# Scan and mixture of experts on one core: the padding write and two half experts' weight loads move back in SyncE's queue

## The chip, the core and the metric

The kernel runs on one core of a Trainium2 chip. The core has five engines that run side by side, each through its own list of instructions in order: TensorE (PE, matrix products), VectorE (DVE), ScalarE (ACT), GpSimd (POOL) and SyncE (SP, which here only issues transfers). Transfers are carried by 16 DMA engines. The metric is the device time of one execution in microseconds (us); lower is better.

## What is computed

The first half is a gated scan over a sequence, the second a mixture of 8 experts, each token going to one expert:

```python
f = lower_bound + (1.0 - lower_bound) / (1.0 + np.exp(-f_logit))
for t in range(S):                        # 4 sequences of S = 5056, D = 256
    h = f[:, t] * h + (1.0 - f[:, t]) * x[:, t];  y[:, t] = h
logits = y @ w_gate;  e_idx = argmax(logits);  gate_w = softmax(logits)[e_idx]
eom = 1.0 / (1.0 + np.exp(-(y @ w_output_gate)))
for e in range(8):                        # N = 20224 tokens, F = 1024
    out[mask] = gate_w * eom[e] * (np.maximum(y[mask] @ w1[e], 0.0) @ w2[e])
```

## The kernel before

The 20224 tokens are cut into chunks of 512, with channels on the partitions. A chunk goes through these steps: load of `f_logit` and `x` (L236, L237, 512 KB each), tanh on ScalarE (L251), a product on VectorE (L255), the forget gate on ScalarE (L260), the scan on VectorE (L266), the norm (L273 and L277), a scale that is a power of two (`pow2`, L142 to L150), the split of the result into two float16 parts (L296 on ScalarE, L300 on VectorE), transposes by DMA into rows of tokens (`turn`, L293, four per chunk, 131 KB each), the gate products on TensorE (L311, L316, tile `pr`), the choice of expert in some twenty small VectorE instructions (from L328, tile `lgo`, to L410, which writes the tokens' factors into the rows), and four scatters by GpSimd (L413) that write the rows to their expert's region of a scratch array in DRAM, `scr`.

The rows of a chunk stand in one of three buffers: chunk 0 has a place of its own (`row0`, lent from the weights' tile `w1s`), odd chunks use `rows1`, even ones `rows0`. Chunk 3's transposes therefore write over the rows that chunk 1's scatters read. Chunk 0's inputs are lent the place `w2s`, chunk 3's the place `w1s`.

The experts' weights come in 16 half experts: `w1` of an expert, then its `w2`. A half is loaded by two transfers of 512 KB (`prep_load`, L546). TensorE forms products of it for its norm (`prep_gram`, L558, 16 products), VectorE takes them up (L565), and a scale follows. ScalarE and VectorE split the half into two float16 parts (L594, L599). The loop over `j` from -2 to 15 takes the halves in order: in step `j` half `j` is split, the products of half `j + 2` are formed and half `j + 3` is loaded. Beside each step some chunk stages run (`step`). As soon as 3 chunks have been scattered, first tiles of 128 tokens of each expert are gathered (`gather`, L607 to L613) and computed on the weights where they stand (L697 and the following); a second such round follows after 5 chunks. Later tiles work on copied weights (L655 and the following).

`padt` is one block of 128 padding rows with factor 0. It is written behind all regions of `scr` at the start (L211); an expert that has fewer than 128 rows yet gathers these rows.

What sets the order: SyncE issues its transfers exactly as the program text has them. For the other four engines, up to a cut, a scheduler orders the instructions by its own estimate of times; so another order in the text, or another place of a load, gives another order on those engines. At most eight of SyncE's transfers are under way: each waits for the one eight places before it.

The part around the change:

```python
    fresh.append(nc.sync.dma_start(out=scr[FREE : FREE + P, :], in_=padt))   # L211
    ...
    for n in range(min(EARLY[0], NCH)):          # L854: chunks 0, 1, 2
        load_chunk(n)
        if n:
            prep_load(n - 1)                     # half experts 0, 1
    for n in range(min(EARLY[0], NCH) - 1, deep):
        prep_load(n)                             # half experts 2, 3
```

Of the kernel before, what the change touches and what calls it, by code (L numbers as in the profile page):

```python
# [27 lines left out]
PERIOD = 8  # L28
# [3 lines left out]
EARLY = (3, 5)  # L32
# [18 lines left out]
def tile_scan_moe(  # L51
# [10 lines left out]
    nc = tc.nc  # L62
    P = 128
# [8 lines left out]
    NCH = -(-N // CH)  # L72
    R = N + P
    FREE = E * R
# [9 lines left out]
    def sure(tokens):  # L84
        """tiles of 256 tokens of one expert that any routing of so many tokens fills beside the first tiles"""
        return max(0, -(-(tokens - len(EARLY) * E * P - E * 255) // 256))
# [9 lines left out]

# [1 line left out]
    ident = cp.tile([P, P], F32, name="ident")  # L98
# [35 lines left out]
    def pow2(ss, t, nm):  # L134
        """from a norm's square: s, a power of two with s times the norm below 2 ** t, and 2 / s"""
        w = ss.shape[1]
        v = sp.tile([P, w], F32, tag=nm + "v", name=nm + "v", bufs=3)
        vi = v.bitcast(I32)
        sc = sp.tile([P, w], F32, tag=nm + "s", name=nm + "s", bufs=3)
        iv = sp.tile([P, w], F32, tag=nm + "i", name=nm + "i", bufs=3)  # L140
        yield SMALL
        nc.vector.tensor_scalar(v, ss, 2.0**-100, 2.0**120, ALU.max, ALU.min)  # L142
        yield SMALL
        nc.vector.tensor_scalar(vi, vi, EXPO, 1, ALU.bitwise_xor, ALU.logical_shift_right)
        yield SMALL
        nc.vector.tensor_scalar(vi, vi, EXPO, None, ALU.bitwise_and)
        yield SMALL
        nc.vector.tensor_scalar(sc, v, 2.0 ** (62 + t), None, ALU.mult)
        yield SMALL
        nc.vector.tensor_scalar(iv.bitcast(I32), sc.bitcast(I32), EXPO, None, ALU.bitwise_xor)  # L150
        return sc, iv

    def together(tasks):
        """a stage of each task: small instructions of VectorE that wait for one another alternate with others"""
        at = {id(g): (g, next(g, None)) for g in tasks}
        last = None
        while True:
            todo = [(g, kind) for g, kind in at.values() if kind]
            if not todo:
                return  # L160
            best = [x for x in todo if x[1] == SMALL and x[0] is not last]
            best = best or [x for x in todo if x[1] == BIG] or todo
            g = best[0][0]
            last = g if best[0][1] == SMALL else None
            del at[id(g)]
            at[id(g)] = (g, next(g, None))

    def alone(g):
        """runs a task to its end; what it returns"""
        while True:  # L170
            try:
                next(g)
            except StopIteration as end:
                return end.value

    # gate weights: the sum of two float16 parts of a scaled value
    gsq = cp.tile([P, KD * G], F32, name="gsq")
# [15 lines left out]

    # writes to rows of their own need no order among them; a reader waits for those it reads
    fresh = []

    def apart(ins, group, keep=()):
        tc.declare_no_dep(raw(ins), group=group, keep=[raw(k) for k in keep], reason="rows apart")
        tc.add_to_no_dep_group(group, raw(ins))

# [1 line left out]
    w1s = cp.tile([P, E, NF, KD, 2, P], F16, name="w1s")  # L202
# [3 lines left out]

    # rows behind each expert's rows: factor 0, an index no scatter takes
    padt = cp.tile([P, RW], I16, name="padt")
    nc.gpsimd.memset(padt, 0)
    nc.gpsimd.iota(padt[:, CM + 2 : CM + 4].bitcast(I32), pattern=[[0, 1]], base=N, channel_multiplier=0)  # L210
    fresh.append(nc.sync.dma_start(out=scr[FREE : FREE + P, :], in_=padt))  # L211
    apart(fresh[0], "scr")
    row2 = [cp.tile([P, NB, RW], I16, name=f"rows{i}") for i in range(2)]
    # the places of the last experts' weights serve the first chunks until then
    top1 = w1f[:, (E - 1) * 2 * WH : E * 2 * WH]
# [6 lines left out]

# [1 line left out]
    state = {"carry": None, "cnt": boff, "sent": boff}  # L224
# [15 lines left out]
    def chunk(c):  # L240
        """the steps of a chunk; each takes from the steps before what other engines made there"""
        t0 = c * CH
# [177 lines left out]

# [1 line left out]
    done0 = cp.tile([P, E], F32, name="done0")  # L422
    nc.gpsimd.memset(done0, 0.0)
    sched = {"done": done0, "new": []}
    slots = []
# [3 lines left out]
    def plan_first():  # L429
        """for each expert: its next 128 rows, or the free rows behind all regions where it has fewer yet"""  # L430
        done = sched["done"]
# [24 lines left out]
    def plan(k, nb, last):  # L456
# [41 lines left out]
        if last:  # L498
            # slots past the last tile take the rows behind expert 0's
            ends = t8("ends", I32)  # L500
# [99 lines left out]

# [1 line left out]
    mpool = {}  # L602
# [85 lines left out]

    # the first tile of an expert: its weights are read where they stand
    def first1(T, h):  # L690
# [46 lines left out]

# [1 line left out]
    prog = {"begun": 0, "tick": 0, "done": 0, "left": 0.0, "planned": 0, "final": False, "got": 0, "rounds": 0}  # L739
# [7 lines left out]
    def loading(c):  # L747
        """the steps of chunk c, with the load of the next once the chunk before has freed its place"""
        at = 0
        for kind in chunk(c):  # L750
            if not kind:
                at += 1
                if at == LOADAT and EARLY[0] <= c + 1 < NCH:
                    load_chunk(c + 1)
            yield kind
# [16 lines left out]
    def pump(tasks, need):  # L772
        """a stage of each chunk under way beside the tasks; every PERIOD stages one more begins"""
        if prog["tick"] <= 0 and prog["begun"] < NCH:
# [37 lines left out]
    def early(j):  # L812
        """half a first tile of an expert ready in step j: what VectorE does, and the rest"""
        if not line or line[0]["half"] == 1 and len(line) == 1:
# [39 lines left out]
    for n in range(min(EARLY[0], NCH)):  # L854
        load_chunk(n)
        if n:
            prep_load(n - 1)
    for n in range(min(EARLY[0], NCH) - 1, deep):
        prep_load(n)
    for j in range(-2, nh):  # L860
        tasks = []
        if 1 <= j < nh + 1 - deep:
            prep_load(j - 1 + deep)
# [28 lines left out]
    def ordered(start, cut):  # L892
        """up to cut the scheduler orders what the engines do, except SyncE"""
        loose = [e.engine for e in (nc.vector, nc.scalar, nc.tensor, nc.gpsimd)]
# [49 lines left out]
    ordered(0, prog["cut"])  # L944
    # the counts may leave the last tiles without a token
    if len(cuts) > 1:
# [43 lines left out]
```

## Time and profile before

| what | value |
|---|---|
| device time, median of 3 runs | 1019.66 us (1018.59 to 1021.29) |
| span of the profiled execution | 1016.9 us |
| busy: TensorE / VectorE / ScalarE / GpSimd | 911.9 / 887.5 / 511.4 / 376.5 us |
| moved by DMA | 146.34 MB, mean 144 GB/s |

The page gives the profiled execution's time as its span, first instruction to last; the runs' median lies 2.8 us above it. In a row of the timeline stand the start (us from the span's start), the time it takes, the engine, the line of the kernel, the operation, what is written and what is read, how often, and in brackets how long the engine had been idle and what ended that. `SPq` and `ACTq` are transfers issued by SyncE and ScalarE; their time is that of the issue, not of the transfer. Matrix products are named PE. `DMA_TRANSPOSE` is a transpose by DMA. In a row of waits stand the waiting instruction, what released it, the time in total, how often, and the longest.

### The profile page before, as it was taken

The numbers are of one execution on the slowest core, as the hardware profiler recorded it, in microseconds if no ns is written. First come the engines' busy times: TensorE is split into PE (matmuls) and PEld (weight loads), VectorE is DVE, ScalarE is ACT, GpSimd is POOL, SyncE is SP. The second block draws the span as 40 slices with busy tenths as digits, with TensorE's granted clock in tenths as the row PEclk, the third lists the DMA queues.
The fourth block names the chain that finished last, engine by engine and source line by source line (L and its number), as shares of the span: only waits on it lengthen the run. The fifth ranks groups of instructions, "written<-read, shape, count | busy, mean of one in ns | idle before, by whom it ended". The sixth has DMA issues, their size and how long they took to land.

```text
span 1016.9 us, 27437 instructions
## 1 busy us (share of the span) xinstructions
PE 911.9 (90%) x9775; PEld 822.8 (81%) x9775; DVE 887.5 (87%) x2803; ACT 511.4 (50%) x1075; POOL 376.5 (37%) x378
## 2 busy tenths in 40 slices
PE   2268998899999999999999999999999999999993
PEld 2157887788888888888888888888888888899993
DVE  7989896899999999999999999999999998758781
ACT  5667774545545555455455554454455543333331
POOL 1523234343444444433444434344444344221221
PEclk9999999999999999999999999999999999999997
DMA  8899966755566565555565565555665534312120
GB/s 309 202 308 287 267 153 154 179 137 138 138 141 151 135 149 153 137 138 137 137 149 141 157 145 132 139 135 132 149 144 152 138 85 104 95 49 45 47 55 16
DMA packets 238547, 146.34 MB, mean 144 GB/s; under 512 B 202558, under 2 KB 204224, under 8 KB 238401
## 3 DMA queue, kind: packets, MB, share of 16 engines
q1 hardware_dynamic: 222752, 101.74, 43.2%
q0 software_dynamic: 15360, 42.74, 13.7%
q8 instruction: 80, 1.31, 0.6%
q14 instruction: 67, 0.54, 0.2%
q10 hardware_dynamic: 288, 0.02, 0.0%
HBM read 58.38 MB, written 44.49 MB: 101 GB/s over the span
## 4 chain that ended last, share of the span: by engine, by line
DVE 54%; issue 17%; DMA 11%; PE 10%; POOL 3%; ACT 2%; SPq 1%; DVEq 1%; POOLq 0%; ACTq 0%
DVE hl L667 11%; DVE xt L266 7%; DVE w L637 5%; DMA rows<-ft 5%; DVE w L643 4%; DVE xt L255 4%; DVE ft L300 3%; POOL out_dram L732 2%; PE ph L655 1%; PE ph L657 1%; PE ph L656 1%; DMA xq<-scr 1%; PE py L685 1%; PE py L687 1%; PE py L686 1%
## 5 line engine op out<-in xcount | busy, mean ns | idle before, releaser
L655 PE MATMUL ph<-xq,w 128*128 128x256 f16 (+1 forms) x1312 | 331.0, 261 | 0.3 <-DVE xv L142 0.3
L657 PE MATMUL ph<-xq,w 128*128 128x256 f16 (+1 forms) x1312 | 331.2, 261 | 0.0
L656 PE MATMUL ph<-xq,w 128*128 128x256 f16 (+1 forms) x1312 | 331.1, 261 | 0.0
L685 PE MATMUL py<-w,hh 128*128 128x256 f16 x1168 | 318.6, 273 | 0.5 <-ACT ft L296 0.3
L687 PE MATMUL py<-w,hl 128*128 128x256 f16 x1168 | 318.6, 273 | 0.0
L686 PE MATMUL py<-w,hh 128*128 128x256 f16 x1168 | 318.5, 273 | 0.0
L732 POOL DMA_INDIRECT out_dram<-yo,mt x146 | 167.9, 1150 | 298.8 <-ACT yo L728 275.1
L413 POOL DMA_INDIRECT scr<-rows,dst x154 | 175.4, 1139 | 229.3 <-issue 215.5
L659 ACT ACTIVATE hh<-ph 128x512 f16<-128x512 f32 (+1 forms) x328 | 178.7, 545 | 153.1 <-PE ph L657 152.8
L667 DVE SCALAR_TENSOR_TENSOR hl<-ph,hh 128x512 f16<-128x512 f32 (+1 forms) x328 | 204.6, 624 | 10.9 <-ACT hh L659 9.1
L655 PEld LDWEIGHTS <-w 128*128 128x128 f16 x1312 | 128.0, 98 | 12.4 <-DVE w L637 0.6
L637 DVE COPY w<-w1s 128x2048 f16 x164 | 115.1, 702 | 26.1 <-PE ph L657 24.7
L657 PEld LDWEIGHTS <-w 128*128 128x128 f16 x1312 | 128.1, 98 | 11.7
L656 PEld LDWEIGHTS <-w 128*128 128x128 f16 x1312 | 128.1, 98 | 11.4
L687 PEld LDWEIGHTS <-hl 128*128 128x128 f16 x1168 | 114.2, 98 | 13.2
L686 PEld LDWEIGHTS <-hh 128*128 128x128 f16 x1168 | 114.2, 98 | 13.2 <-issue 0.8
L685 PEld LDWEIGHTS <-hh 128*128 128x128 f16 x1168 | 114.2, 98 | 12.5
L643 DVE COPY w<-w2s 128x2048 f16 x164 | 111.8, 682 | 0.5 <-PE py L687 0.3
L260 ACT ACTIVATE ft<-ft,fb,fa 128x512 f32<-128x512 f32 (+1 forms) x76 | 60.6, 807 | 100.7 <-DVE xt L255 98.0
L296 ACT ACTIVATE ft<-xt,sa 128x512 f16<-128x512 f32 (+1 forms) x76 | 50.2, 708 | 106.1 <-DVE li L285 101.9
L266 DVE TENSOR_TENSOR_SCAN xt<-ft,xt 128x512 f32<-128x512 f32 (+4 forms) x78 | 90.7, 1170 | 0.0
L728 ACT ACTIVATE yo<-py,fac 128x256 f32<-128x256 f32 x146 | 61.6, 465 | 26.4 <-PE py L687 25.7
(178 smaller groups left out, 1311.5 us busy)
## 6 DMA issues: line engine op xcount, KB each, us to landing
ft<-in_fT_dram SPq DMA_DIRECT2D x37, 512.0 KB
xt<-in_xT_dram SPq DMA_DIRECT2D x37, 512.0 KB
w<-in_wT_dram SPq DMA_DIRECT2D x32, 512.0 KB
scr<-rows,dst POOLq DMA_INDIRECT x154, 3.3
rows<-ft SPq DMA_TRANSPOSE x152
out_dram<-yo,mt POOLq DMA_INDIRECT x146, 2.8
xq<-scr SPq DMA_TRANSPOSE x99
scr<-padt SPq DMA_DIRECT2D x9, 136.0 KB
```

Of the source, the lines that this page charges most:

```text
L266: nc.vector.tensor_tensor_scan(out=xt[:, k, a:z], data0=ft[:, k, a:z], data1=xt[:, k, a:z], initial=init, op0=ALU.mult, op1=ALU.add)
L413: ins = nc.gpsimd.indirect_dma_start(out=scr[:, :], out_offset=IOA(ap=dst[:, b : b + 1], axis=0), in_=rows[:, b, :], in_offset=None)
L637: nc.vector.tensor_copy(out=w, in_=w1f[:, ds(T["ev"] * (2 * WH) + h * 2 * QH, 2 * QH)])
L655: nc.tensor.matmul(out=o, lhsT=w[:, f, k, 0, :], rhs=T["xh"][:, k, 0:n], start=first, stop=False)
L656: nc.tensor.matmul(out=o, lhsT=w[:, f, k, 0, :], rhs=T["xl"][:, k, 0:n], start=False, stop=False)
L657: nc.tensor.matmul(out=o, lhsT=w[:, f, k, 1, :], rhs=T["xh"][:, k, 0:n], start=False, stop=last)
L659: nc.scalar.activation(hh[:, :, 0:n], ph[:, :, 0:n], AF.Relu)
L667: nc.vector.scalar_tensor_tensor(out=hl[:, :, 0:n], in0=ph[:, :, 0:n], scalar=0.0, in1=hh[:, :, 0:n], op0=ALU.max, op1=ALU.subtract)
L685: nc.tensor.matmul(out=o, lhsT=hh[:, i, c], rhs=w[:, f, 0, :], start=first, stop=False, skip_group_check=True)
L686: nc.tensor.matmul(out=o, lhsT=hh[:, i, c], rhs=w[:, f, 1, :], start=False, stop=False, skip_group_check=True)
L687: nc.tensor.matmul(out=o, lhsT=hl[:, i, c], rhs=w[:, f, 0, :], start=False, stop=last, skip_group_check=True)
L732: ins = nc.gpsimd.indirect_dma_start(out=out[:, :], out_offset=IOA(ap=T["mt"][:, b, 2:4].bitcast(I32), axis=0), in_=T["yo"][:, b, :], in_o ...
```

## The change

The padding write moves from ahead of the first loads to behind them. The loads of half experts 2 and 3 move from ahead of the loop into its steps -1 and 0. Some texts in quotes or comments are gone as well; they make no instruction. Two lines fewer stand ahead of most of the code, so L236 of before is L234 now, L293 is L291, L410 is L408, L599 is L597, and so on.

```diff
@@ the padding block
     nc.gpsimd.iota(padt[:, CM + 2 : CM + 4].bitcast(I32), pattern=[[0, 1]], base=N, channel_multiplier=0)
-    fresh.append(nc.sync.dma_start(out=scr[FREE : FREE + P, :], in_=padt))
-    apart(fresh[0], "scr")
@@ ahead of the loop, and its first lines
         load_chunk(n)
         if n:
             prep_load(n - 1)
-    for n in range(min(EARLY[0], NCH) - 1, deep):
-        prep_load(n)
+    fresh.append(nc.sync.dma_start(out=scr[FREE : FREE + P, :], in_=padt))
+    apart(fresh[0], "scr")
     for j in range(-2, nh):
         tasks = []
-        if 1 <= j < nh + 1 - deep:
+        if -1 <= j < nh + 1 - deep:
             prep_load(j - 1 + deep)
```

The front of SyncE's queue before, up to the first transposes (`w` is a weight buffer, `w2s`, `ft` and `xt` the places of chunks' inputs):

```order
L211 DMA scr<-padt 128x544
L236 DMA w2s<-in_fT_dram 128x2x512
L237 DMA w2s<-in_xT_dram 128x2x512
L236 DMA ft<-in_fT_dram 128x2x512
L237 DMA xt<-in_xT_dram 128x2x512
L546 DMA w<-in_wT_dram 128x1024 x2
L236 DMA ft<-in_fT_dram 128x2x512
L237 DMA xt<-in_xT_dram 128x2x512
L546 DMA w<-in_wT_dram 128x1024 x6
L293 DMA_TRANSPOSE w1s<-w2s 128x4x128 x4
```

and now:

```order
L234 DMA w2s<-in_fT_dram 128x2x512
L235 DMA w2s<-in_xT_dram 128x2x512
L234 DMA ft<-in_fT_dram 128x2x512
L235 DMA xt<-in_xT_dram 128x2x512
L544 DMA w<-in_wT_dram 128x1024 x2
L234 DMA ft<-in_fT_dram 128x2x512
L235 DMA xt<-in_xT_dram 128x2x512
L544 DMA w<-in_wT_dram 128x1024 x2
L856 DMA scr<-padt 128x544
L291 DMA_TRANSPOSE w1s<-w2s 128x4x128 x4
```

The padding write went behind the weights, and four of the eight weight transfers left the front.

They stand again further on in SyncE's queue. Before, from the transposes of chunk 1 (`rows_133`) over those of chunk 2 (`rows_132`) and chunk 3 (`rows_133` again, from `w1s`) to the first gather (`xq`):

```order
L293 DMA_TRANSPOSE rows_133<-ft 128x4x128 x4
L293 DMA_TRANSPOSE rows_132<-ft 128x4x128 x4
L236 DMA ft<-in_fT_dram 128x2x512
L237 DMA xt<-in_xT_dram 128x2x512
L293 DMA_TRANSPOSE rows_133<-w1s 128x4x128 x4
L236 DMA ft<-in_fT_dram 128x2x512
L237 DMA xt<-in_xT_dram 128x2x512
L546 DMA w<-in_wT_dram 128x1024 x2
L607 TENSOR_LOAD pf_tab
L607 ISA x2
L610 ISA
L610 DMA_TRANSPOSE xq<-scr 128x4x128
```

and now, up to half expert 4 (chunk 1's and 3's rows are `rows_132` here, chunk 2's `rows_131`):

```order
L291 DMA_TRANSPOSE rows_132<-ft 128x4x128 x2
L544 DMA w<-in_wT_dram 128x1024 x2
L291 DMA_TRANSPOSE rows_132<-ft 128x4x128 x2
L291 DMA_TRANSPOSE rows_131<-ft 128x4x128 x4
L234 DMA ft<-in_fT_dram 128x2x512
L235 DMA xt<-in_xT_dram 128x2x512
L291 DMA_TRANSPOSE rows_132<-w1s 128x4x128 x2
L544 DMA w<-in_wT_dram 128x1024 x2
L291 DMA_TRANSPOSE rows_132<-w1s 128x4x128 x2
L234 DMA ft<-in_fT_dram 128x2x512
L235 DMA xt<-in_xT_dram 128x2x512
L544 DMA w<-in_wT_dram 128x1024 x2
```

Half expert 2 now stands in the midst of chunk 1's transposes and half expert 3 in the midst of chunk 3's, ahead of chunk 5's load and the first gather.

VectorE around the factors of chunk 0 (L410 before; it writes into the rows that GpSimd scatters first). Before:

```order
L300 SCALAR_TENSOR_TENSOR ft<-xt,sa,ft 128x512 x2
L340 TENSOR_REDUCE mx<-lgo 128x4
L404 SCALAR_TENSOR_TENSOR fc<-es,eg 128x4
L396 TENSOR_REDUCE dst<-pos 128x4
L343 TENSOR_TENSOR dl<-lgo,mx 128x32
L408 RECIPROCAL fc<-fc 128x4
L346 SCALAR_TENSOR_TENSOR key<-dl,rev 128x32
L410 TENSOR_SCALAR w1s<-fc,xi 128x4
L352 TENSOR_REDUCE km<-key 128x4
L399 TENSOR_REDUCE es<-ex 128x4
L255 SCALAR_TENSOR_TENSOR w1s<-w1s 128x512 x2
```

and now (L253, L264, L298, L326 and L408 are L255, L266, L300, L328 and L410 of before):

```order
L298 SCALAR_TENSOR_TENSOR ft<-xt,sa,ft 128x512 x2
L353 TENSOR_TENSOR oh<-key,km 128x32
L402 SCALAR_TENSOR_TENSOR fc<-es,eg 128x4
L264 SCALAR_TENSOR_TENSOR w1s<-w1s,xt 128x512 x2
L356 TENSOR_TENSOR og<-oh,lgo 128x32
L406 RECIPROCAL fc<-fc 128x4
L563 SCALAR_TENSOR_TENSOR jk,l_624<-pg,ident 128x128
L381 TENSOR_TENSOR pos<-pk,cnt 128x32
L387 TENSOR_TENSOR cnt<-cnt,pk 128x8
L326 TENSOR_TENSOR lgo<-lgp 128x64
L359 TENSOR_REDUCE gs<-og 128x4
L408 TENSOR_SCALAR w1s<-fc,xi 128x4
```

Chunk 0's factors now stand behind chunk 3's two scans (L264), behind the norm of half expert 2 (L563) and behind the first step of chunk 2's choice (L326); chunk 3's L253 pair stands ahead of these rows as well. On TensorE the 16 products of half expert 2 stand, in the new order, behind the first two of chunk 2's gate products and ahead of the others.

## The prediction

> **What bounds the kernel now.** I read the page first, for how busy the engines are over the span.
>
> ```profile
> span 1016.9 us, 27437 instructions
> PE   2268998899999999999999999999999999999993
> DVE  7989896899999999999999999999999998758781
> ...
> w<-in_wT_dram SPq DMA_DIRECT2D x32, 512.0 KB
> ```
>
> Each digit is 25.4 us. From the eighth slice on TensorE is at 9 of 10 and VectorE as well; in the first two slices TensorE is at 2 and VectorE nearly full. The order of the instructions of VectorE, ScalarE, TensorE and GpSimd differs from before only in the start, up to the first tiles of the later phase. So the change is decided in the first 60 us, and by how much of what it does there is still there at 180 us. The times by stretch (engine busy us, then clock, DMA share, GB/s) say what is short there.
>
> ```profile
> 10.00:19.00 9.00, 2.40 (x20) 1.86 (x19) 8.05 (x23) 7.79 (x17) 0.00 (x0) 1.00 1.04 417
> 23.00:26.00 3.00, 1.96 (x25) 1.80 (x23) 3.00 (x10) 1.38 (x5) 0.00 (x0) 1.00 1.40 208
> 26.00:30.00 4.00, 2.31 (x39) 2.04 (x35) 3.93 (x22) 3.49 (x8) 0.00 (x0) 1.00 1.02 278
> 30.00:38.00 8.00, 1.58 (x22) 1.07 (x23) 8.00 (x35) 5.12 (x12) 3.50 (x3) 1.00 1.06 164
> 60.00:110.00 50.00, 43.03 (x581) 40.26 (x581) 45.70 (x146) 35.38 (x61) 15.17 (x14) 0.97 1.07 288
> 110.00:160.00 50.00, 45.58 (x657) 42.39 (x654) 43.58 (x145) 35.49 (x63) 20.44 (x20) 1.00 0.73 189
> 160.00:180.00 20.00, 16.29 (x217) 15.14 (x217) 13.02 (x54) 9.17 (x19) 7.95 (x8) 0.91 0.83 169
> ```
>
> VectorE (third pair) is the full engine from 10 to 38 us; the DMA engines are full too. Then SyncE's queue in order of time, which holds the moved transfers:
>
> ```profile
> 3.16 0.38 SPq L211 DMA_DIRECT2D scr<-padt  x1
> 3.60 0.42 SPq L236 DMA_DIRECT2D w2s<-in_fT_dram  x1
> 7.77 6.55 SPq L546 DMA_DIRECT2D w<-in_wT_dram  x6
> 19.40 5.30 SPq L293 DMA_TRANSPOSE w1s<-w2s  x4
> 24.75 0.57 SPq L236 DMA_DIRECT2D w1s<-in_fT_dram  x1
> 25.93 10.89 SPq L293 DMA_TRANSPOSE rows<-ft  x8
> 37.01 0.44 SPq L236 DMA_DIRECT2D ft<-in_fT_dram  x1
> 46.35 5.15 SPq L293 DMA_TRANSPOSE rows<-w1s  x4
> 51.61 0.52 SPq L236 DMA_DIRECT2D ft<-in_fT_dram  x1
> 53.04 0.93 SPq L546 DMA_DIRECT2D w<-in_wT_dram  x2
> 55.08 1.21 SPq L610 DMA_TRANSPOSE xq<-scr  x1
> ...
> SPq L293 <- DMA scr<-rows,dst: 8.2, 2, 6.8
> SPq L211 <- POOL rows L378: 2.7, 1, 2.7
> POOL scr L413 <- DMA rows<-ft: 30.5, 1, 30.5
> ```
>
> Two waits matter. The queue's first instruction, the padding write, waits 2.7 us for GpSimd's constants, and everything behind it starts at 3.60. And between 37.98 and 46.35 the queue stands still: chunk 3's transposes write the row buffer that chunk 1's scatters read, so they wait for those scatters (8.2 us). Behind them, in order, stand chunk 5's load (51.61) and the first gather (55.08), with which the experts' work begins. The engines that feed this path:
>
> ```profile
> 0.83 0.38 ACTq L122 DMA_DIRECT2D lbt<-in_lbT_dram  x1
> 4.60 0.15 DVE L148 TENSOR_SCALAR gts<-gtv 128x1 f32<-128x1 f32 x1
> 5.13 0.25 DVE L190 SCALAR_TENSOR_TENSOR wgs<-wgc,gts,wgs 128x32 f16<-128x32 f32 x1
> 9.03 1.29 DVE L255 SCALAR_TENSOR_TENSOR w2s<-w2s 128x512 f32<-128x512 f32 x2 [3.65 <-DMA w2s<-in_xT_dram]
> 14.44 1.28 DVE L266 TENSOR_TENSOR_SCAN xt<-ft,w2s,xt 128x512 f32<-128x512 f32 x1 [0.31 <-ACT ft L260]
> 25.23 0.20 DVE L328 TENSOR_TENSOR lgo<-lgp 128x64 f32<-128x64 f32 x1
> 32.73 0.22 DVE L410 TENSOR_SCALAR w1s<-fc,xi 128x4 f32<-128x4 f32 x1
> 33.05 1.28 DVE L255 SCALAR_TENSOR_TENSOR w1s<-w1s 128x512 f32<-128x512 f32 x2
> 33.88 1.46 POOL L413 DMA_INDIRECT scr<-w1s,dst  x1 [30.48 <-DMA rows<-ft]
> 34.71 1.27 DVE L266 TENSOR_TENSOR_SCAN w1s<-w1s,xt 128x512 f32<-128x512 f32 x1
> 36.25 1.28 DVE L266 TENSOR_TENSOR_SCAN w1s<-w1s,xt 128x512 f32<-128x512 f32 x1
> 39.86 0.96 POOL L413 DMA_INDIRECT scr<-rows,dst  x1 [0.30 <-issue]
> 43.66 1.15 POOL L413 DMA_INDIRECT scr<-rows,dst  x1 [0.30 <-issue]
> 58.06 0.69 DVE L255 SCALAR_TENSOR_TENSOR xt<-ft,xt 128x512 f32<-128x512 f32 x1 [1.09 <-ACT ft L251]
> 61.10 0.26 PE L697 MATMUL ph<-xq,w1s 128*128 128x128 f16 x1 [3.56 <-DMA xq<-scr]
> ```
>
> Chunk 0's rows are complete when VectorE has written their factors (L410, until 32.95); GpSimd's first scatter starts at 33.88, chunk 1's follow without a pause (39.86 to 44.81), and the transposes are let go at 46.35. That is a chain VectorE, GpSimd, SyncE, and not one of the moved transfers is in it.
>
> **The change part by part.** *The padding write* leaves the front. The first load can be issued when ScalarE's queue issues its first one, at 0.83, instead of 3.60: 2.77 us earlier. Its own 0.38 us of issue lies behind the weights of half expert 1, where the queue has nothing to do until 19.40; without that cover it costs 0.38. Its first reader is the gather, at 55.
>
> *VectorE's order at the start.* The gate weights' small instructions (L142 to L190) ran while VectorE waited for the first chunk (the 3.65 of idle before L255). Now they stand between its large ones, up to the first scan of chunk 1. From L148 to the end of L190 is 5.38 - 4.60 = 0.78; three more stand singly, some 0.1 each by the spacing below. So that scan comes at 14.44 - 2.77 + 1.0 = 12.7, which is 1.7 earlier. The same gain holds up to chunk 0's L328: 25.23 becomes 23.5.
>
> *VectorE's order behind it.* In the new order chunk 3's L255 pair and its two scans stand ahead of chunk 0's factors, where they stood behind, with eight more small instructions. From the rows: the pair takes 1.28, the scans 2 x 1.2 (1.27 each, overlapping the next by 0.07), and 34 small ones took (32.73 - 25.23) less 2 x 1.2 of weights and 1.3 of subtractions, 3.8 or 0.11 each, so eight are 0.9. Together 4.6, less the 1.7 gained: the factors come 2.9 later, at 35.6.
>
> *The two half experts moved back.* Half expert 2's two transfers now stand behind the first two transposes of chunk 1, and TensorE's 16 products on them stand ahead of the rest of chunk 2's gate products, for which VectorE's L328 of chunk 2 waits, and behind this in VectorE's order are chunk 0's factors. Before, no such wait was there. Issue: 25.93 - 1.7 + 2 x 1.36 (eight transposes in 10.89) = 27.0. In the ring stand ahead of it chunk 3's 1.05 MB from about 24.7 on (3.8 us at 278 GB/s) and two transposes of 0.13 MB (1.6 us at 164), and it has 1.05 MB itself (2.5 us at 417): it lands at 32.6, with the products 34 to 35. VectorE gets there at about 35. So between 0 (covered by VectorE's large instructions) and, with its bytes at 164 GB/s, 6.4 - 2.5 = 3.9 us later, less the 1 in hand, 2.9. I take 0.1, being nearest to the covered case. Slip of the first scatter: 3.0.
>
> The early issue also had a use: the 6.55 us of six issues lay under a time when nothing else wanted the ring. The Trainium skill, in "DMA: Bandwidth & Descriptors", section "Rules for kernel authors", says to issue a transfer early, compute, and wait for it late. The 417 GB/s row agrees that the early weights were hidden; by that rule alone this part can only cost, between the 0 and the 2.9 above.
>
> *SyncE's queue from there.* The transposes of chunk 3 go at 46.35 + 3.0 = 49.4, and half expert 3's two issues (0.93) now stand in their midst. Chunk 5's load and the first gather come 3.9 later: 55.5 and 59.0. VectorE idled 1.09 for that load at 58.06; it has the same work ahead of it in the new order, so it waits some 3 us longer. TensorE's first expert product goes from 61.10 to about 65.
>
> *What reaches the end.* Between 60 and 180 TensorE is busy 104.9 of 120 us and VectorE 102.3, so there is room to catch up 15 us, but only where what they wait for does not come late too; the gathers and the loads all stand in the same queue, shifted. Bounds: nothing (0) and all (3.9). I take three quarters, 2.9, nearest to a queue in which all is shifted. Behind 180 us the orders are the same, and a shift stays. Sum against the execution's own span: 1016.9 + 2.9 = 1019.8; the median of the runs, 1019.66, is 2.8 above the span, so 1022.6. About 0.3% (3.1 us) is what can be told from no change here.
>
> **The rivals.** *The early start carries through (not slower).* The profile puts GpSimd's 30.5 us of wait down to the transposes, not to VectorE. If they are what the scatter waits for, taking four transfers (2.1 MB, 5.0 us at 417 GB/s) out of their way gains between the 1.7 of the early start and 5.0: 1014.7 to 1018.0, middle 1016.3. It decides if the last transpose of chunk 0 lands behind L410. Against it: in 23 to 26 us the rate falls to 208 GB/s, the transposes are running there, and L410 ends only at 32.95. The Trainium skill, same page, section "Queues, rings and completion order", has descriptors consumed in ring order on each engine. By it the transposes, issued at 19.40, had to wait for all the weights ahead; the trace agrees, with the full rate until 19 and the drop at 23.
>
> *The slip is absorbed.* VectorE is idle 7.0 of the 20 us from 160 to 180; if that idle time ends with something that does not move, the end stays: 1019.7. Against it: the same queue order there.
>
> *The late weights decide.* With the 2.9 of the bound instead of 0.1, and all carried: 3.9 + 2.8 = 6.7, 1026.4. For it: the DMA engines are over-full in 23 to 38 us. Against it: VectorE's own work of 4.6 us covers most.
>
> **How the numbers follow.** Forecast, the slipped scatter: 0.48, with its own range 1020 to 1025 and half of it over the 3.1. Early start: 0.28, of which 0.17 faster by over 3.1 us. Absorbed: 0.12. Late weights: 0.12. So faster 0.17, within 0.3% 0.11 + 0.24 + 0.12 = 0.47, slower 0.24 + 0.12 = 0.36. The range goes from the early start's middle to the late weights' time: 1016 to 1026.5.
>
> **What would show it.** Right: first load issued near 0.8, chunk 1's first scan near 12.7, chunk 0's factors written near 35.6, the first scatter near 36.9, chunk 3's transposes near 49.4, the first expert product near 65, and a larger wait of VectorE for chunk 5. Early start: the first scatter ahead of 33. Late weights: TensorE waiting for a weight transfer ahead of chunk 2's gate products, and the first scatter behind 39. Absorbed: all that, but the first products on copied weights (L655) at their old time. It is wrong if the first scatter is late and the end is early: then what I take for the path of the start isn't the one that sets its end.

## The result, and the profile after

| | before | the change |
|---|---|---|
| device time, median of 4 runs each | 1019.12 us (1017.92 to 1021.29) | 1034.78 us (1032.84 to 1034.92) |
| span of the profiled execution | 1016.9 us | 1031.1 us |

The ratio is 1.0137, 95% interval 1.0106 to 1.0168. The quotient of the two medians is 1.0154, which lies inside the interval. The change is slower by 14 us by the ratio and by 15.7 us by the medians, where 2.9 were forecast and 6.7 was the worst case. The page of the changed kernel, its span and the busy tenths in slices of 25.8 us:

```profile
span 1031.1 us, 27435 instructions
PE   2147898799999999999999999999999999999993
DVE  8868886799999999999999999999999998767781
```

The third to the seventh slice of TensorE read 47898 where before had 68998, and VectorE's second and third read 86 where before had 98. Busy time by stretch, in the columns of the prediction (TensorE first, VectorE third):

```profile
60.00:110.00 50.00, 35.71 (x451) 32.58 (x451) 38.80 (x130) 30.35 (x50) 12.94 (x14) 0.93 1.00 283
110.00:160.00 50.00, 43.88 (x635) 41.31 (x633) 41.10 (x134) 32.03 (x57) 16.11 (x16) 0.97 0.88 222
160.00:180.00 20.00, 19.37 (x255) 17.84 (x255) 15.26 (x48) 12.59 (x26) 7.60 (x8) 0.91 0.55 140
```

From 60 to 160 us TensorE is busy for 9.0 us less than before (79.59 against 88.61) and VectorE for 9.4 less. So work is put off here, behind the stretch that the prediction looked at. SyncE's queue up to the first gather, from the timeline of the changed kernel:

```profile
0.83 0.45 SPq L234 DMA_DIRECT2D w2s<-in_fT_dram  x1
16.88 5.25 SPq L291 DMA_TRANSPOSE w1s<-w2s  x4
49.70 2.50 SPq L291 DMA_TRANSPOSE rows<-w1s  x2
52.25 1.09 SPq L544 DMA_DIRECT2D w<-in_wT_dram  x2
53.44 3.47 SPq L291 DMA_TRANSPOSE rows<-w1s  x2
57.00 0.59 SPq L234 DMA_DIRECT2D ft<-in_fT_dram  x1
61.63 1.22 SPq L608 DMA_TRANSPOSE xq<-scr  x1
```

And the engines that it feeds, from the same timeline (start us, duration us, engine and line, in brackets the idle time before and what ended it):

```profile
11.92 1.28 DVE L264 TENSOR_TENSOR_SCAN xt<-ft,w2s,xt 128x512 f32<-128x512 f32 x1
35.66 0.22 DVE L408 TENSOR_SCALAR w1s<-fc,xi 128x4 f32<-128x4 f32 x1
36.81 1.14 POOL L411 DMA_INDIRECT scr<-w1s,dst  x1 [33.38 <-DVE mx L338]
58.98 1.03 PE L556 MATMUL pg<-w 128*128 128x128 bf16 x8 [5.60 <-DMA w<-in_wT_dram]
61.63 0.29 DVE L563 SCALAR_TENSOR_TENSOR jk<-pg,ident 128x128 f16<-128x128 f32 x1 [5.16 <-PE pg L556]
64.75 1.29 DVE L253 SCALAR_TENSOR_TENSOR xt<-ft,xt 128x512 f32<-128x512 f32 x2 [0.53 <-DMA xt<-in_xT_dram]
67.80 0.27 PE L695 MATMUL ph<-xq,w1s 128*128 128x128 f16 x1 [5.13 <-DMA xq<-scr]
```

Up to 50 us this is the forecast to within 0.8 us. Then comes what it did not have: TensorE waits 5.60 us for half expert 3, VectorE 5.16 behind it, and the first gather is 6.55 us late (61.63 against 55.08) instead of 3.9.

That is not yet 14. How the delay grows is seen at VectorE's counts, one per chunk (`cnt`, L389 before, L387 in the change), which place the chunk's tokens in their regions. Start in us, from the timeline:

| chunk | 3 | 4 | 5 | 6 | 7 | 8 |
|---|---|---|---|---|---|---|
| before | 52.49 | 72.87 | 101.50 | 125.35 | 148.75 | 167.62 |
| the change | 53.63 | 81.73 | 110.79 | 143.44 | 163.81 | 185.63 |
| later by | 1.1 | 8.9 | 9.3 | 18.1 | 15.1 | 18.0 |

Behind the counts of chunk 8 the plan of the later tiles is made (`pl_n` and what follows), and their gathers wait for it. The instructions that write `pl_n`, before (count, shortest/median/longest ns, first and last start):

```profile
L466 DVE TENSOR_TENSOR pl_n<-cnt,boff x33: 156/157/161, 169.1 to 868.9; 128x8 f32<-128x8 f32 x33
```

and in the change:

```profile
L464 DVE TENSOR_TENSOR pl_n<-cnt,boff x33: 155/157/168, 186.0 to 883.0; 128x8 f32<-128x8 f32 x33
```

The first plan is 16.9 us late, the last one 14.1, the end 14.2. From the first plan to the end it is 847.8 us before and 845.1 now. So the question is what makes chunk 8's counts late. The delay jumps at chunk 4 (by 7.8 us) and at chunk 6 (by 8.8).

### The profile page after: what moved, and what is told of

Its sections match the earlier page's. It is cut to its first block, busy times and chain, and to the rows that moved or that the text cites. A ratio compares the mean times of both kernels' runs of the same rounds, so it can differ in the third digit from the quotient of the medians.

```text
span 1031.1 us, 27435 instructions
## 1 busy us (share of the span) xinstructions
PE 915.2 (89%) x9775; PEld 825.0 (80%) x9775; DVE 889.1 (86%) x2803; ACT 510.9 (50%) x1075; POOL 377.5 (37%) x378
## 5 line engine op out<-in xcount | busy, mean ns | idle before, releaser
L411 POOL DMA_INDIRECT scr<-rows,dst x154 | 177.7, 1154 | 230.4 <-issue 222.5
L657 ACT ACTIVATE hh<-ph 128x512 f16<-128x512 f32 (+1 forms) x328 | 178.7, 545 | 157.8 <-PE ph L655 157.8
L665 DVE SCALAR_TENSOR_TENSOR hl<-ph,hh 128x512 f16<-128x512 f32 (+1 forms) x328 | 204.8, 624 | 14.1 <-ACT hh L657 12.3
L654 PEld LDWEIGHTS <-w 128*128 128x128 f16 x1312 | 128.5, 98 | 14.2 <-issue 2.5
L655 PEld LDWEIGHTS <-w 128*128 128x128 f16 x1312 | 128.4, 98 | 12.1
L635 DVE COPY w<-w1s 128x2048 f16 x164 | 114.8, 700 | 25.8 <-PE ph L655 24.4
L685 PEld LDWEIGHTS <-hl 128*128 128x128 f16 x1168 | 114.3, 98 | 13.3
L264 DVE TENSOR_TENSOR_SCAN xt<-ft,xt 128x512 f32<-128x512 f32 (+4 forms) x78 | 90.6, 1170 | 0.0
```

Of the source, the lines that this page charges most:

```text
L411: ins = nc.gpsimd.indirect_dma_start(out=scr[:, :], out_offset=IOA(ap=dst[:, b : b + 1], axis=0), in_=rows[:, b, :], in_offset=None)
L635: nc.vector.tensor_copy(out=w, in_=w1f[:, ds(T["ev"] * (2 * WH) + h * 2 * QH, 2 * QH)])
L654: nc.tensor.matmul(out=o, lhsT=w[:, f, k, 0, :], rhs=T["xl"][:, k, 0:n], start=False, stop=False)
L655: nc.tensor.matmul(out=o, lhsT=w[:, f, k, 1, :], rhs=T["xh"][:, k, 0:n], start=False, stop=last)
L657: nc.scalar.activation(hh[:, :, 0:n], ph[:, :, 0:n], AF.Relu)
L665: nc.vector.scalar_tensor_tensor(out=hl[:, :, 0:n], in0=ph[:, :, 0:n], scalar=0.0, in1=hh[:, :, 0:n], op0=ALU.max, op1=ALU.subtract)
```

## The experiments

Each ratio below is to the kernel before on the same chip. On the chip of the first four kernels the kernel before took 1029.2 us, on those of the others 1019.7 to 1020.2; so between chips only ratios are compared. All kernels compute the whole result. Each trace shows one execution.

### The parts of the change, one at a time

The first theory was "late weights": half experts 2 and 3 land late and their readers hold up all that is behind them.

Only the padding write moved (half experts 2 and 3 in front, behind it):

```diff
-    fresh.append(nc.sync.dma_start(out=scr[FREE : FREE + P, :], in_=padt))   # ahead of the loads
...
+    fresh.append(nc.sync.dma_start(out=scr[FREE : FREE + P, :], in_=padt))   # behind half expert 1
+    for n in (2, 3):
+        prep_load(n)
```

> Only the padding write moves, behind the weights of half expert 1; half experts 2 and 3 stay ahead of the first transposes. The instructions of VectorE at the start are ordered anew here too (the gate weights' small ones between the first large ones). Theory 'late weights' (the time goes to half expert 3, and less to half expert 2, landing late, with TensorE and VectorE waiting for them): no weight lands late here, so 1015 to 1020, about the time before. Rival 'new start' (the earlier first load and the new order of the first instructions alone lose the time, by putting the queues out of step): 1028 or more. Rival 'slipped scatter' of the prediction: as the first, for chunk 0's factors need not wait for chunk 3's scans here; first scatter at or ahead of 34.

Measured: 1.0040 (1.0022 to 1.0058).

Only the two loads moved:

```diff
-    for n in range(min(EARLY[0], NCH) - 1, deep):
-        prep_load(n)
...
-        if 1 <= j < nh + 1 - deep:
+        if j + 3 in (2, 3) or 1 <= j < nh + 1 - deep:
             prep_load(j - 1 + deep)
```

> Only the loads of half experts 2 and 3 move, into the same places as in the change; the padding write stays first in the queue. Theory 'late weights': 1032 to 1037, like the change or up to 2.8 above it, since the first load is again at 3.6; TensorE waits over 4 us for half expert 3's bytes near 60 us. Rival 'new start': 1017 to 1023, since the start is that of before. Rival 'slipped scatter': the first scatter 3 us late or more and an end of 1022 to 1026.

Measured: 1.0105 (1.0077 to 1.0134).

The padding moved, half expert 2 in front, half expert 3 late:

```diff
+    for n in (2,):
+        prep_load(n)
...
+        if j + 3 in (3,) or 1 <= j < nh + 1 - deep:
```

> The change, but half expert 2 stays ahead of the first transposes: only half expert 3 is loaded in the midst of chunk 3's transposes. Theory 'late weights': most of the loss stays, 1027 to 1035, with a wait of TensorE for its bytes of 4 us or more near 58 us, though the first scatter is at most 1 us late. Rival 'slipped scatter' (chunk 0's factors behind half expert 2's products): no loss, 1016 to 1020.

Measured: 1.0072 (1.0045 to 1.0098).

The padding moved, half expert 3 in front, half expert 2 late:

```diff
+    for n in (3,):
+        prep_load(n)
...
+        if j + 3 in (2,) or 1 <= j < nh + 1 - deep:
```

> The change, but half expert 3 stays ahead of the first transposes: only half expert 2 is loaded in the midst of chunk 1's transposes. Theory 'late weights': half expert 2 had cost 1 us of VectorE's wait in the change, so 1017 to 1022. Rival 'slipped scatter': 1022 to 1034, the scatter of chunk 0 being late by 2 to 3 us and the loss growing from there. If this one and the one with half expert 3 late both lose little, the two add up through the queue's issue slots rather than by one late transfer.

Measured: 1.0123 (1.0092 to 1.0154).

The times that these four expectations name are for a chip on which before takes 1019.7 us; here they are read as ratios to that. "Late weights" fails. The kernel without any late weight is slower than before too (no range that was said for it holds 1.0040), and the one with half expert 3 in front, said to be at 0.997 to 1.002, loses 1.23%. The kernel with both loads late comes to 1.05% where 1.2 or more were said, a miss within the noise, but its TensorE waits 3.0 us for half expert 3 and not over 4. Only half expert 3 late gives 1.0072, the lower edge of what "late weights" said, with a wait of 2.28 us where 4 or more were said.

"Slipped scatter" holds half expert 2's 1.0123 in its range, but not by its mechanism: the first scatter is at 32.81 there, earlier than before (33.88). With both loads late it is at 39.01, 5.1 us late, and the loss is larger than said. "New start" fails on both its numbers.

In the kernel with half expert 3 in front and half expert 2 late, the timeline shows a long pause of VectorE at a norm, and a late first gather:

```profile
38.75 0.29 DVE L565 SCALAR_TENSOR_TENSOR jk<-pg,ident 128x128 f16<-128x128 f32 x1 [3.14 <-remote]
59.24 1.21 SPq L610 DMA_TRANSPOSE xq<-scr  x1
```

The profile does not name what ended this pause ("remote"), and it is not shown to be a wait for the weights: TensorE waited 1.20 us for them and had done all 32 products on both half experts by 35.2:

```profile
31.84 2.21 PE L558 MATMUL pg<-w 128*128 128x128 bf16 x19 [1.20 <-DMA w<-in_wT_dram]
34.02 1.19 PE L558 MATMUL pg<-w 128*128 128x128 bf16 x13
```

With only half expert 3 late, on the other hand, TensorE waits for it and the first gather is still no later than before (55.08), by the timeline of that kernel:

```profile
52.02 1.03 PE L558 MATMUL pg<-w 128*128 128x128 bf16 x8 [2.28 <-DMA w<-in_wT_dram]
54.36 1.21 SPq L610 DMA_TRANSPOSE xq<-scr  x1
```

The ratios by themselves would add up within the noise: 0.40% for the padding, 0.32 more for half expert 3 and 0.83 more for half expert 2 make 1.55%, and the change has 1.37. But each of the four kernels moves transfers and has the four engines' instructions ordered anew with them, and the padding's 0.40% comes without any transfer that lands late. So the order became the suspect, and the next kernels part the two.

### The order without the transfers, the transfers without the order

These kernels fix the order on VectorE, ScalarE, TensorE and GpSimd up to the cut (530, 196, 1652 and 92 instructions) by a list that stands in the kernel, where the scheduler had chosen. SyncE's queue is not bound by it.

```diff
+        given = pinned() if cut else []          # by engine: places in the text's order
+        for e, seq in zip(loose, given):
+            own = [ins for ins in every[:cut] if ins.engine == e]
+            for p, q in zip(seq[:-1], seq[1:]):
+                tc.add_manual_dep(own[q], own[p].name, AFTER, reason="order")
```

The transfers of before, the change's order (the text of before with that list):

> The transfers of before, in their old order (padding first, all four half experts ahead of the first transposes), with VectorE, ScalarE, TensorE and GpSimd held to the order of instructions that the change has. No weight lands late. Theory 'order' (the new order of the first 180 us loses the time by itself, whatever lands when): ratio 1.007 or more to before, the fourth gather at 91 us or later. Theory 'waits' (the time is lost in waiting for half experts 2 and 3 to land): ratio under 1.003, the fourth gather near 86 to 88, as only the slip of chunk 0's factors is left.

Measured: 1.0127 (1.0102 to 1.0153). The first gather on SyncE's queue, from the timeline:

```profile
60.30 1.34 SPq L610 DMA_TRANSPOSE xq<-scr  x1
```

and of the same kernel the instructions that write `pl_n`:

```profile
L466 DVE TENSOR_TENSOR pl_n<-cnt,boff x33: 154/157/160, 182.8 to 882.4; 128x8 f32<-128x8 f32 x33
```

The order by itself gives nearly the whole loss, with every weight in place early. The fourth gather came at 93.55, as "order" said. In this trace the four engines' instructions of the first 240 us stand in the order of the change, one by one; and as the ratio is that of the change, holding an order by a list costs nothing that shows.

The change's transfers and order, with half expert 3 issued ahead of chunk 4's load:

```diff
-        if -1 <= j < nh + 1 - deep:
+        if j == -1 or 1 <= j < nh + 1 - deep:
             prep_load(j - 1 + deep)
...
+            if (j, z) == (-1, 1):
+                prep_load(3)
```

> The change with its order of instructions kept on the four engines; only half expert 3's two loads are moved in SyncE's queue, from the midst of chunk 3's transposes (which wait for chunk 1's scatters) to ahead of chunk 4's load, where the queue stands still later on. They should land near 43 us. Theory 'waits': TensorE's 5.6 us and VectorE's 5.2 us of wait near 60 us go, and the ratio falls from 1.0137 to 1.007 or less. Theory 'order': the ratio stays at 1.010 or more, though the wait is gone.

Measured: 1.0172 (1.0146 to 1.0198). TensorE's wait for half expert 3 is gone, and the timeline shows another on VectorE:

```profile
48.35 1.29 DVE L255 SCALAR_TENSOR_TENSOR xt<-ft,xt 128x512 f32<-128x512 f32 x2 [5.70 <-DMA xt<-in_xT_dram]
```

and of the same kernel the instructions that write `pl_n`:

```profile
L466 DVE TENSOR_TENSOR pl_n<-cnt,boff x33: 154/157/161, 194.2 to 891.3; 128x8 f32<-128x8 f32 x33
```

The weights now stand ahead of chunk 4's load, which lands 5.4 us later than in the change (VectorE took it up at 42.97 there). The "order" theory's 1.010 or more holds. That the kernel would be slower than the change was in neither theory.

The same transfers with before's order, but for the products on half experts 2 and 3 and their norms, which stand where the bytes should be there:

> The transfers of the run with half expert 3 ahead of chunk 4's load (padding behind, half experts 2 and 3 behind chunk 1's first and chunk 2's last transposes), with the order of instructions of before on all four engines, but for the 2 x 16 products on half experts 2 and 3 and the two VectorE instructions of their norms, which stand later: behind chunk 1's counts and behind chunk 3's gate products. Theory 'order': ratio 0.996 to 1.003. Theory 'waits': the same, if the places are late enough for the bytes. Rival 'bytes' (late weights slow the transposes, chunk loads and scatters beside them): 1.005 or more, with transposes and chunk 4's load slower than in the other runs.

Measured: 1.0053 (1.0037 to 1.0069). VectorE at chunk 4's load, from the timelines of before and of this kernel:

```profile
42.69 1.29 DVE L255 SCALAR_TENSOR_TENSOR xt<-ft,xt 128x512 f32<-128x512 f32 x2 [1.49 <-DMA xt<-in_xT_dram]
47.16 1.29 DVE L255 SCALAR_TENSOR_TENSOR xt<-ft,xt 128x512 f32<-128x512 f32 x2 [8.32 <-DMA xt<-in_xT_dram]
```

and of the same kernel the instructions that write `pl_n`:

```profile
L466 DVE TENSOR_TENSOR pl_n<-cnt,boff x33: 154/157/161, 175.7 to 875.2; 128x8 f32<-128x8 f32 x33
```

Against the kernel just above only the order differs, and 1.2% of the time goes. But "order" had said 1.003 at most, and "bytes" said 1.005 or more. VectorE waits 8.32 us for chunk 4 (1.49 before) and takes it up 4.5 us later than before (47.16 against 42.69); chunk 3's counts behind it are 4.7 us late, the first gather 5.10 (60.18), the plan 6.6. This is the "bytes" rival's sign for chunk 4's load. That the transposes were slower, as it also said, is not shown, and the later place of the 32 products was not tried alone; TensorE had no wait for half expert 3 there.

Only the padding write moved, before's order kept:

> Only the padding write moves, as in the run with the padding alone, but with before's order of instructions on all four engines. Theory 'order': the 2 to 2.8 us of the earlier start last, since no instruction is ordered anew: ratio 0.996 to 0.999. If the run with the padding alone lost its time through timing and not through the new order of the start, this one loses it as well: 1.002 to 1.006.

Measured: 0.9974 (0.9960 to 0.9989), 1017.99 us against 1020.06: faster than before and than the change. SyncE's first load and first gather, from the timeline:

```profile
0.82 0.45 SPq L236 DMA_DIRECT2D w2s<-in_fT_dram  x1
52.84 1.21 SPq L610 DMA_TRANSPOSE xq<-scr  x1
```

and of the same kernel the instructions that write `pl_n`:

```profile
L466 DVE TENSOR_TENSOR pl_n<-cnt,boff x33: 153/157/161, 168.5 to 868.4; 128x8 f32<-128x8 f32 x33
```

The early start is worth 2.1 us by the medians and 2.7 by the ratio (1.1 to 4.1) where nothing is ordered anew. With the scheduler's new order the same move of one transfer cost 0.40%.

### Where in the order

Lists were put together from the two orders: one up to a point, the rest as the other has it.

The change's order to 58 us, then before's; transfers of before:

> The transfers of before. The four engines follow the change's order up to the norm of half expert 3 (the first 182 of VectorE's 530 ordered instructions, 146 of TensorE's 1652, 60 of ScalarE's 196: what the change had done by 58 us), and before's order behind it. Theory 'tail' (the loss comes from the order behind 58 us, where the chunks' steps stand later between the first experts' tiles): the first gather near 60 as with the whole new order, the plan of the later tiles at 176 or earlier instead of 183, ratio 1.003 to 1.006. Theory 'head' (the late chunk 0 to 3 set everything behind them): plan at 180 or later, ratio 1.010 or more.

Measured: 1.0040 (1.0022 to 1.0058). The first gather, from the timeline:

```profile
60.37 1.33 SPq L610 DMA_TRANSPOSE xq<-scr  x1
```

and of the same kernel the instructions that write `pl_n`:

```profile
L466 DVE TENSOR_TENSOR pl_n<-cnt,boff x33: 154/157/163, 178.2 to 878.1; 128x8 f32<-128x8 f32 x33
```

Before's order to 54 us, then the change's:

> The transfers of before. The four engines follow before's order up to 54 us (176 of VectorE's 530 ordered instructions, 163 of TensorE's 1652, 60 of ScalarE's 196) and the change's order behind it. Theory 'tail': the first gather at 55 as before, but the plan of the later tiles at 177 or later instead of 169, ratio 1.007 or more. Theory 'head': plan at 172 or earlier, ratio under 1.003.

Measured: 1.0099 (1.0065 to 1.0134). The first gather, from the timeline:

```profile
55.58 1.21 SPq L610 DMA_TRANSPOSE xq<-scr  x1
```

and of the same kernel the instructions that write `pl_n`:

```profile
L466 DVE TENSOR_TENSOR pl_n<-cnt,boff x33: 154/156/161, 181.2 to 879.6; 128x8 f32<-128x8 f32 x33
```

The larger part is in the tail: the first gather is late by 0.5 us, the plan by 12.1. Head and tail together give 1.39%, the whole order 1.27%. One thing of "tail" missed: the plan of the head's execution was at 178.2, not 176 or earlier. That execution is the slowest of its ten (1027.86 us, the median is 1024.73), so the ratio says more than this plan.

The change's transfers, its order to 58 us, then before's:

> The transfers of the change, and its order of instructions up to the norm of half expert 3; behind it before's order. Half expert 3 still lands late and TensorE still waits for it near 59 us, so the first gather stays near 61.6. Theory 'tail': of the 16.9 us by which the plan of the later tiles is late in the change 6 to 9 are left, ratio 1.006 to 1.009. Theory 'head': ratio 1.012 or more.

Measured: 1.0045 (1.0027 to 1.0063). TensorE's wait for half expert 3, from the timeline:

```profile
59.39 1.03 PE L558 MATMUL pg<-w 128*128 128x128 bf16 x8 [4.91 <-DMA w<-in_wT_dram]
```

and of the same kernel the instructions that write `pl_n`:

```profile
L466 DVE TENSOR_TENSOR pl_n<-cnt,boff x33: 154/157/161, 178.7 to 878.4; 128x8 f32<-128x8 f32 x33
```

TensorE still waits 4.91 us for half expert 3, and the time is that of the head with all weights in front, 1.0040. So with this order the moved transfers, early start and late weights together, are worth about nothing (0.05%, each ratio being good to 0.18), and a different order behind 58 us takes two thirds of the change's loss away. The loss is smaller than either theory said, 1.006 being the least; the plan is 9.6 us late where 6 to 9 were said, but this execution too is the slowest of its ten (1028.14, median 1024.68).

Before's order to 54 us, the change's to about 119, then before's:

> The transfers of before, before's order up to 54 us, the change's order from there to about 119 us (342 of VectorE's ordered instructions, 787 of TensorE's, 120 of ScalarE's), and before's order again behind it. It parts the tail's loss in two: chunk 4's counts (4 us late there) and chunk 6's gate products and counts (8 us more). If chunk 6's place is the larger part, its first scatter comes by 137 instead of 145, the plan of the later tiles by 175 instead of 181, and the ratio falls from 1.0099 to 1.003 to 1.006. If the loss is made ahead of 119 us and only shows later, the ratio stays at 1.008 or more.

Measured: 1.0047 (1.0029 to 1.0065); the first plan was at 175.7, chunk 6's first scatter at 137.71, each 0.7 us behind what was said for the case of chunk 6. So about half of the tail's loss is made from 54 to 119 us, and half behind that. The counts say where: in the tail chunk 6's and chunk 8's are 13.3 us later than before; here they are 7.3 and 6.7. The second half is there by chunk 6. In this kernel chunk 4's counts are 3.5 us late and chunk 5's 4.9.

In the timeline of before, VectorE's way from chunk 6's logits (L328) to its one-hot choice (L355), its counts, and GpSimd's first scatter:

```profile
111.59 0.23 DVE L328 TENSOR_TENSOR lgo<-lgp 128x64 f32<-128x64 f32 x1 [0.19 <-ACT lgp L324]
116.15 0.18 DVE L355 TENSOR_TENSOR oh<-key,km 128x32 bf16<-128x32 f32 x1
125.35 0.16 DVE L389 TENSOR_TENSOR cnt<-cnt,pk 128x8 f32<-128x8 f32 x1
130.45 1.09 POOL L413 DMA_INDIRECT scr<-rows,dst  x1 [0.30 <-issue]
```

The same in the change, with the large instructions that stand ahead of it and in its midst:

```profile
123.89 1.29 DVE L597 SCALAR_TENSOR_TENSOR w1s<-w,ws,w1s 128x1024 f16<-128x1024 f32 x1
125.36 1.28 DVE L597 SCALAR_TENSOR_TENSOR w1s<-w,ws,w1s 128x1024 f16<-128x1024 f32 x1
126.56 0.22 DVE L326 TENSOR_TENSOR lgo<-lgp 128x64 f32<-128x64 f32 x1
130.69 0.21 DVE L627 TENSOR_SCALAR fac<-mt,cinv 128x1 f32<-128x1 f32 x1 [3.85 <-DMA mt<-scr]
136.38 1.28 DVE L253 SCALAR_TENSOR_TENSOR xt<-ft,xt 128x512 f32<-128x512 f32 x2
139.52 0.17 DVE L353 TENSOR_TENSOR oh<-key,km 128x32 bf16<-128x32 f32 x1
143.44 0.15 DVE L387 TENSOR_TENSOR cnt<-cnt,pk 128x8 f32<-128x8 f32 x1
150.06 1.93 POOL L411 DMA_INDIRECT scr<-rows,dst  x1 [3.26 <-issue]
```

Before, the logits stood ahead of the split of a half expert (L599, at 113.29 and 114.86 there), and the choice came 4.6 us behind them. In the change they stand behind that split (L597, the first two rows), and between logits and choice stand a wait of 3.85 us for a gathered tile's factors (L627), two more instructions of a split and the next chunk's products: 13.0 us. The logits are 15.0 us late, the choice 23.4, the counts 18.1. From the logits to the counts in the change VectorE is idle for only 5.2 of 16.9 us: it is at work, on other things first. What each of these pieces costs was not tried one by one.

### The end follows the first plan

First plan (us from the start) and span of the profiled executions:

| kernel | first plan | span | between |
|---|---|---|---|
| padding moved, order kept | 168.5 | 1016.4 | 847.9 |
| before | 169.1 | 1016.9 | 847.8 |
| order of the change from 54 to 119 us | 175.7 | 1023.0 | 847.3 |
| weights late, before's order | 175.7 | 1023.3 | 847.6 |
| head of the order | 178.2 | 1026.2 | 848.0 |
| transfers of the change, head | 178.7 | 1026.4 | 847.7 |
| tail of the order | 181.2 | 1027.6 | 846.4 |
| order alone | 182.8 | 1030.4 | 847.6 |
| the change | 186.0 | 1031.1 | 845.1 |
| half expert 3 ahead of chunk 4 | 194.2 | 1039.3 | 845.1 |

What is lost up to the plan is lost at the end, but for 3 us of 17 or 25. Each row is one execution, so a row's times can lie some us beside its kernel's median: the first two rows are 0.5 us apart, their medians 2.1. The four kernels of the slower chip are left out; there 847.7 to 851.5 us lie between plan and end.

## Why the prediction was wrong

The direction was right, the size was not: 1019.8 us of span were forecast (2.9 more than before), and 1031.1 came (14.2 more).

**Right, to the start of chunk 3's transposes, in part by luck.** First load 0.83 (said 0.8), chunk 1's first scan 11.92 (12.7), chunk 0's factors 35.66 (35.6), first scatter 36.81 (36.9), transposes 49.70 (49.4). The slip came through VectorE's order, as the step on the order said. That the factors came out to 0.1 us is luck, for two errors cancel. The scan was 0.8 us earlier than said: the gate's small instructions, priced at 1.0, added 0.5 between VectorE's first large instruction and that scan, and that first one came 0.2 earlier than said. And VectorE waited 0.97 us for half expert 2's products, where 0.1 was taken for the first scatter and none for the factors. The rival that had the transposes decide is answered by the scatter's row: what released it was VectorE.

**Half expert 3 was under-sized.** The step on SyncE's queue counted its two issues, 0.93 us, and not the arrival of its bytes; half expert 2 alone got bounds. TensorE waited 5.60 us for it. The first gather came at 61.63 instead of 59.0 and the first expert product at 67.80 instead of 65, but not because TensorE waited: on SyncE's queue the two transposes behind the weights took 3.47 us in the place of about 2.5, and the gather then waited 0.9 us, until 61.50, for chunk 2's last scatter, which GpSimd had issued at 53.37. Whether half expert 3's bytes held that scatter up was not tried; with all weights early and the same order the gather came at 60.30. The wait named for chunk 5 became smaller, 0.53, since VectorE stood behind the weights already. But this is not where the 14 us went: with before's order behind 58 us the wait stays and the ratio is that without it (1.0045 and 1.0040).

**The failed step: "So the change is decided in the first 60 us".** The prediction said that the orders differ up to the first tiles of the later phase, which begin at 183 us. It then looked at the first 60 us alone and priced the rest as a share of the slip: "three quarters, 2.9", between bounds of nothing and all. A new order has no such bounds. It puts each chunk's steps at other places between the first experts' tiles, and from 54 us on it alone costs 0.99%. The stretch that was costed, the change's transfers with its order up to 58 us, costs 0.45%, or 4.6 us (2.8 to 6.4), against the 2.9 that were said for it. The "room to catch up 15 us" on TensorE was not used, and from 60 to 160 us it did 9.0 us less. The first plan needs chunk 8's counts, and these come when VectorE's order brings them, behind other chunks' and tiles' instructions and the waits of those.

**Right again: "Behind 180 us the orders are the same, and a shift stays"**, by the last table.

**The rivals.** "The early start carries through" holds as a mechanism, 0.26%, where the order is kept; in the change the new order covers it. "The slip is absorbed" is out: the first products on copied weights started at 197.5 instead of 183.2, and the end is late as well. "The late weights decide" is out by the two heads, though waits for weights were there (3.18 us of TensorE for half expert 2 as well); its sign, the first scatter behind 39, did not come. The Trainium skill's rule in "DMA: Bandwidth & Descriptors", "Rules for kernel authors", to issue early and wait late, points the right way on the wait of 5.60 us. No run shows that this wait costs the end anything.

**Open.** Why the scheduler's estimate turns a small move at the front into another order 100 us later was not tried. Nor was it parted which of the pieces between 54 and 119 us cost the first half of the tail. And the two loads, moved without any new order into the places that the change gives them, were not run; the nearest is late weights at another place, 1.0053.

## What to carry to other kernels

Where a scheduler orders the instructions, a moved transfer is two changes: the transfer, and a new order as far as the scheduler reaches. Price both over that whole stretch, by following what all later work waits for (here chunk 8's counts) back through each engine's order, and not by the engines' busy time. When such a change disappoints, run the new order with the old transfers and the old order with the new ones first; here that took a gain of 0.26% out of a move that had measured as a loss of 0.40%.

## What the runs showed of the hardware that was not expected

A pair of 512 KB loads put ahead of another load cost more than its bytes would at the start's rate (an estimate of 2.5 us at 417 GB/s). With half expert 3's 1.05 MB ahead of chunk 4's load, VectorE took that load up 5.4 us later than in the change. 2.1 us of this are a later issue (39.38 against 37.28), of which 1.2 are the issue of the weights themselves; the other 3.3 us would be some 320 GB/s for the 1.05 MB, an estimate. From 38 to 48 us all DMA engines together moved 313 GB/s there and 203 in the change. In the change the same 1.05 MB, issued at 52.25, had its first half in use at 58.98 and its second at 60.56. That a load waits for the bytes issued ahead of it agrees with the Trainium skill, "DMA: Bandwidth & Descriptors", "Queues, rings and completion order", which has descriptors consumed in ring order on each DMA engine.

The kernel before took 1029.2 us on one chip and 1019.1 to 1020.2 on the others (medians), 1% apart. A ratio of 1.004 can be read only between runs on one chip.
